# Moving w1's load behind the first tiles of x, two evacuations to VectorE, and splitting the last tile, in a one-core token-mixer and MLP kernel

## The chip, the cores and the metric

The kernel runs on one core of one Trainium2 chip. The metric is device microseconds of that core: the median of repeated executions, lower is better. A trace covers the span of one execution, some 1.8 us less than its time (155.1 of 156.92 us in the traced run of the changed kernel). The granted clock is the share of TensorE's full clock that the profile says was granted. PE is TensorE, PEld its weight loads, DVE is VectorE, ACT is ScalarE, POOL is GpSimd, SP is SyncE; in a timeline "SPq" and "ACTq" are DMA issues of those engines.

## The reference

```python
B, S, D, F = 1, 2048, 512, 1792                  # x, w1..w4 in bf16
h  = gelu(layernorm(x) @ w1)
# four channel groups of h are shifted along S by +1, -1, +2, -2 and put together again: hs
x1 = x + hs @ w2
out = x1 + gelu(layernorm(x1) @ w3) @ w4
```

## The kernel before

x is worked on in 16 tiles of 128 rows. In layer 1 each tile goes through these steps: statistics on DVE (bn_stats, bn_aggr), 1/sqrt of the variance (tiles 0 to 3 on ACT and DVE; later pairs of tiles on GpSimd as `vpe` and `rstd`), normalization on DVE (`norm`), transposition on PE (`htp`), and evacuation of the transposed tile out of PSUM, into which the kernel has PE write, into `xnT` (`hev`). Four such tiles feed one group of PE matmuls (`yg`), whose result ACT copies out of PSUM; DVE then does most of the gelu. The kernel gives each engine its list in a fixed order. The order is worked out when the kernel is built, from estimated durations:

```python
class Sched:
    def add(self, eng, name, fn, reads=(), writes=(), dur=100.0, queue=None): ...
    def merge(self): ...   # list scheduling by `dur`; gives one order, waits are put in from reads and writes
```

These are the loads and their gates. `after` names what must be done before the load is issued:

```python
add_w_dma("act", "w1", w1_sb, w1, D * D * 2)               # ACT's queue, first of all
for t in range(min(4, NT)):
    add_x_dma("sp", t, 1)                                  # tiles 0..3, one load each
for k in range(1, NST):
    add_x_dma("sp", 4 * k, 4)                              # tiles 4..7, 8..11, 12..15
add_w_dma("pool", "w2", w2_sb, w2, D * D * 2, after=[(("xT", min(5, NT - 1)), 1)])
add_w_dma("pool", "w3", w3_sb, w3, D * F * 2, after=[(("xT", NT - 1), 1)])
add_w_dma("pool", "w4", w4_sb, w4, D * F * 2, after=[(("x1", ORDER2[min(4, NT - 1)]), 0)])
```

So w2 is issued by GpSimd, in its ordinary instruction list, once the evacuation of tile 5 is done. In that list it stands ahead of the `vpe` and `rstd` of tiles 8 and 9.

The evacuation of transposed tiles, and the last stage (14 matmuls for each tile, evacuation with the residual on DVE, store):

```python
def add_head_evac(t):
    ...
    sc.add("act", f"hev{t}", lambda e: e.activation(xnT[:, :, P * t : P * (t + 1)], src, ACT_F.Copy),
           reads=res, writes=[(("xT", t), 1)], dur=600)
# mm4: o_ps[128x512] = sum over 14 of h2T(fc).T @ w4(fc); then o_sb = o_ps + x1 on DVE; then the store from SP
```

## Time and profile before

| | before |
|---|---|
| time, median | 159.43 us (159.11 to 160.69, 16 runs) |
| span of the traced run | 157.7 us |
| busy: PE, DVE, ACT, POOL | 86%, 78%, 57%, 13% |
| granted clock | 1.0 |

The busy shares are averages over stages with different limits. The next lines are from the busy table over stretches of the kernel before. Its columns are the stretch in us, its length, the busy us of each engine (with the number of instructions), the granted clock, the busy share of the DMA engines, and GB/s.

```profile
8.00:26.00 18.00, 15.31 (x97) 7.71 (x99) 16.19 (x47) 12.30 (x21) 7.07 (x13) 1.00 0.18 69
26.00:62.00 36.00, 30.91 (x143) 13.33 (x147) 34.72 (x87) 25.75 (x35) 10.80 (x18) 1.00 0.54 141
62.00:85.00 23.00, 20.89 (x94) 8.80 (x93) 22.58 (x25) 20.35 (x17) 0.00 (x1) 1.00 0.16 32
85.00:152.00 67.00, 66.47 (x303) 30.02 (x309) 45.40 (x55) 29.70 (x25) 0.00 (x0) 1.00 0.08 28
```

From 26 to 85 us DVE is busy 57.3 of 59 us and sets the pace. From 85 us on it is PE, busy 66.5 of 67 us. Between 8 and 26 us DVE is busy 16.2 of 18 us; most of what is missing there is one wait. The waits of DVE in the kernel before (columns: who waited for whom, us in total, times, longest):

```profile
DVE o_sb L527 <- PE o_ps L612: 23.1, 11, 2.6
DVE st L376 <- DMA x_sb<-in_x_dram: 5.1, 2, 4.0
DVE xn_buf L425 <- POOL rstd L416: 2.2, 3, 1.4
```

The first line belongs to the end, where DVE has time. The second, 5.1 us for x tiles, lies in the first 6 us, before DVE has anything to work on. The third, 2.2 us for `rstd`, lies where DVE sets the pace. The head of the kernel before as a timeline (start us, duration, engine, line, operation, out<-in, count, and in brackets the idle time before it and what ended it):

```profile
4.04 0.69 DVE L376 BATCH_NORM_STATS2 st<-x_sb 128x6 f32<-128x512 bf16 x1 [4.04 <-DMA x_sb<-in_x_dram]
5.80 0.69 DVE L376 BATCH_NORM_STATS2 st<-x_sb 128x6 f32<-128x512 bf16 x1 [1.07 <-DMA x_sb<-in_x_dram]
...
8.08 0.38 DVE L425 TENSOR_SCALAR xn_buf<-x_sb,mv,rstd 128x512 bf16<-128x512 bf16 x1
...
9.56 1.28 DVE L376 BATCH_NORM_STATS2 st<-x_sb 128x6 f32<-128x512 bf16 x2
...
11.42 3.35 PE L574 MATMUL y_ps<-xnT,w_sb 128*128 128x512 bf16 x8 [0.90 <-ACT xnT L558]
...
17.12 0.96 POOL L350 DMA_DIRECT2D w_sb<-in_w_dram  x1 [2.86 <-ACT xnT L558]
...
18.11 0.25 POOL L411 TENSOR_SCALAR vpe<-mv 128x2 f32<-128x2 f32 x1
...
18.44 0.72 POOL L416 TENSOR_TENSOR rstd<-vpe,neghalf 128x2 f32<-128x2 f32 x1
...
19.19 0.74 DVE L425 TENSOR_SCALAR xn_buf<-x_sb,mv,rstd 128x512 bf16<-128x512 bf16 x2 [1.38 <-POOL rstd L416]
```

Tile 0 lands at 4.04 us. Tile 1 was issued 0.46 us later and is used 1.76 us later. The first norm starts at 8.08 us, the statistics of tile 4 at 9.56 us, the first y matmuls at 11.42 us; those eight matmuls take 3.35 us. GpSimd gets to issue w2 at 17.12 us, after 2.86 us of waiting for the evacuation of tile 5. Only then does it compute the `rstd` of tiles 8 and 9, and DVE idles 1.38 us for it.

### The profile page before, as it was taken

How to read it: one execution, taken by the hardware profiler on the slowest of the kernel's cores; microseconds unless marked ns; L12 is line 12 of the kernel's file. 1: busy time of each engine (PE TensorE's matmuls, PEld its weight loads, DVE VectorE, ACT ScalarE, POOL GpSimd, SP SyncE). 2: the span in 40 equal slices, each digit the busy share in tenths (PEclk: the TensorE clock that was granted, in tenths of full speed). 3: DMA queues.
4: the chain of work that ended last, by engine and by line, in shares of the span. 5: the costliest groups of instructions: out<-in, count | busy, mean ns of one | idle time of the engine just before them, and what ended most of it. 6: DMA issues, size and time to landing. Idle time of an engine off the chain costs nothing.

```text
span 157.7 us, 1812 instructions
## 1 busy us (share of the span) xinstructions
PE 136.3 (86%) x643; PEld 60.9 (39%) x656; DVE 123.0 (78%) x220; ACT 89.9 (57%) x98; POOL 19.7 (13%) x46
## 2 busy tenths in 40 slices
PE   0069889659969999995999999999999999999992
PEld 0044344214324444442443444444444444444440
DVE  0799699999999998999999999613999938922311
ACT  3074777979956555789896979610687742200000
POOL 4013642200144446000000000000000000000000
PEclk9999999999999999999999999999999999999999
DMA  5940120480069845530000010001000010110010
GB/s 148 325 192 0 48 85 6 111 354 0 2 205 294 170 70 100 100 63 0 0 2 0 0 35 2 0 33 37 34 33 0 0 67 33 37 67 33 33 66 34
DMA packets 13433, 11.12 MB, mean 70 GB/s; under 512 B 9137, under 2 KB 12209, under 8 KB 13425
## 3 DMA queue, kind: packets, MB, share of 16 engines
q1 hardware_dynamic: 12016, 6.29, 15.3%
q0 software_dynamic: 880, 4.19, 7.8%
q10 hardware_dynamic: 528, 0.52, 1.0%
q8 instruction: 5, 0.08, 0.2%
q14 instruction: 4, 0.02, 0.1%
HBM read 6.82 MB, written 2.10 MB: 57 GB/s over the span
## 4 chain that ended last, share of the span: by engine, by line
PE 44%; DVE 12%; issue 3%; ACT 2%; POOL 1%; POOLq 1%
PE o_ps L612 30%; PE y_ps L574 13%; DVE ub L477 3%; DVE x2b L462 3%; DVE h2T L497 2%; ACT ysb L449 2%; DVE x2b L469 2%; DVE xn_buf L425 1%; POOL vpe L411 1%; POOLq L728 1%; DVE st L376 1%; DVE o_sb L527 0%; DVE mv L381 0%; ACT sgb L484 0%
## 5 line engine op out<-in xcount | busy, mean ns | idle before, releaser
L574 PE MATMUL y_ps<-xnT,w_sb 128*128 128x512 bf16 x283 | 66.0, 385 | 5.1 <-ACT ysb L449 3.8
L612 PE MATMUL o_ps<-w_sb,h2T 128*128 128x512 bf16 x218 | 48.5, 379 | 0.3
L449 ACT ACTIVATE ysb<-y_ps 128x1024 bf16<-128x1024 f32 x36 | 35.6, 1018 | 18.5 <-DVE h2T L497 12.1
L484 ACT ACTIVATE sgb<-ub 128x1024 bf16<-128x1024 bf16 (+1 forms) x24 | 35.6, 1485 | 14.1 <-DVE ub L477 14.1
L574 PEld LDWEIGHTS y_ps<-xnT,w_sb 128*128 128x128 bf16 x288 | 27.3, 99 | 40.5 <-issue 5.1
L612 PEld LDWEIGHTS o_ps<-w_sb,h2T 128*128 128x128 bf16 x224 | 21.9, 98 | 26.4
L527 DVE TENSOR_TENSOR o_sb<-o_ps,x_sb 128x512 bf16<-128x512 f32 x16 | 11.0, 690 | 23.2 <-PE o_ps L612 23.1
L376 DVE BATCH_NORM_STATS2 st<-x_sb 128x6 f32<-128x512 bf16 x32 | 20.3, 672 | 5.1 <-DMA x_sb<-in_x_dram 5.1
L477 DVE TENSOR_TENSOR ub<-x2b,ysb 128x1024 bf16<-128x1024 bf16 (+1 forms) x24 | 23.0, 958 | 0.8
L462 DVE TENSOR_TENSOR x2b<-ysb 128x1024 bf16<-128x1024 bf16 (+1 forms) x24 | 22.8, 951 | 0.2
L497 DVE TENSOR_TENSOR h2T<-ysb,sgb 128x2048 bf16<-128x2048 bf16 (+1 forms) x16 | 17.2, 1085 | 0.0
L594 PE MATMUL o_ps<-w_sb,hT 128*128 128x512 bf16 x62 | 16.0, 379 | 0.1
L469 DVE TENSOR_SCALAR x2b<-x2b 128x1024 bf16<-128x1024 bf16 (+1 forms) x24 | 13.6, 565 | 0.8
L425 DVE TENSOR_SCALAR xn_buf<-x_sb,mv,rstd 128x512 bf16<-128x512 bf16 x32 | 11.7, 408 | 2.4 <-POOL rstd L416 2.2
L548 PE MATMUL o_ps<-ident,xn_buf 128*128 128x128 bf16 x56 | 5.1, 231 | 9.7 <-DVE xn_buf L425 8.5
L519 ACT ACTIVATE x_sb<-o_ps 128x512 bf16<-128x512 f32 x16 | 9.5, 597 | 5.8 <-PE o_ps L594 5.7
L416 POOL TENSOR_TENSOR rstd<-vpe,neghalf 128x2 f32<-128x2 f32 x14 | 10.5, 753 | 1.2
L558 ACT ACTIVATE xnT<-o_ps 128x512 bf16<-128x512 bf16 x14 | 7.6, 597 | 2.5 <-PE o_ps L548 2.3
L594 PEld LDWEIGHTS o_ps<-w_sb,hT 128*128 128x128 bf16 x64 | 6.3, 98 | 6.9
L590 PE MATMUL o_ps<-x_sb,ident 128*128 128x512 bf16 x16 | 6.1, 382 | 3.2 <-DVE hT L512 3.2
L548 PEld LDWEIGHTS o_ps<-ident,xn_buf 128*128 128x128 bf16 x56 | 3.7, 102 | 12.7 <-DVE xn_buf L425 9.5
L411 POOL TENSOR_SCALAR vpe<-mv 128x2 f32<-128x2 f32 x14 | 4.5, 320 | 20.3 <-DVE mv L381 20.3
(21 smaller groups left out, 24.0 us busy)
## 6 DMA issues: line engine op xcount, KB each, us to landing
w_sb<-in_w_dram POOLq DMA_DIRECT2D x2, 1792.0 KB, 8.3
out_dram<-o_sb SPq DMA_DIRECT2D x16, 128.0 KB, 1.8
x_sb<-in_x_dram SPq DMA_DIRECT2D x3, 512.0 KB, 6.7
w_sb<-in_w_dram ACTq DMA_DIRECT2D x1, 512.0 KB, 4.7
x_sb<-in_x_dram SPq DMA_DIRECT2D x4, 128.0 KB, 4.4
w_sb<-in_w_dram POOLq DMA_DIRECT2D x1, 512.0 KB, 4.3
xnT<-xn_buf SPq DMA_TRANSPOSE x16, 2.5
```

The lines of the kernel that those rows point to most:

```text
L376: sc.add("dve", f"bnst{gt}", lambda e: e.bn_stats(st6[:, gt, :], src), reads=[(rsrc, 0)], writes=[(("st6", gt), 0)], dur=650)
L425: lambda e: e.tensor_scalar(xn_buf[:, gt % NXN, :], src, mv[:, gt, 0:1], rstd[:, gt : gt + 1], ALU.subtract, ALU.mult),
L449: lambda e: e.activation(ysb[:, u % NYS, GW * h : GW * (h + 1)], y_ps[:, 512 * b : 512 * b + GW], ACT_F.Copy),
L462: lambda e: e.tensor_tensor(x2b[:, u % NX2, 0:W], y, y, ALU.mult),
L469: lambda e: e.tensor_scalar(x2, x2, GELU_K, None, ALU.add),
L477: lambda e: e.tensor_tensor(ub[:, u % NUU, 0:W], x2b[:, u % NX2, 0:W], y, ALU.mult),
L484: lambda e: e.activation(sgb[:, u % NSS, 0:W], ub[:, u % NUU, 0:W], ACT_F.Sigmoid, scale=GELU_C2),
L497: sc.add("dve", f"c4_{u}", lambda e: e.tensor_tensor(dst, y, sg, ALU.mult), reads=rd, writes=w, dur=90 + 0.54 * W)
L527: lambda e: e.tensor_tensor(o_sb[:, k % NO, :], o_ps[:, 512 * (k % 2) : 512 * (k % 2 + 1)], x1_sb[:, t, :], ALU.add),
L574: ins = e.matmul(dst, wsb[:, dc, P * fc : P * (fc + 1)], srcT[:, dc, 512 * st : 512 * (st + 1)], start=(dc == 0), stop=(dc == DC - 1))
L594: ins = e.matmul(dst, hT[:, j, c0 : c0 + P], w2_sb[:, j, :], start=False, stop=(j == DC - 1))
L612: ins = e.matmul(dst, h2T[:, fc, st2 % 2, P * q : P * (q + 1)], w4_sb[:, fc, :], start=(fc == 0), stop=(fc == FC - 1))
```

## The change

The intent is a quicker head and a shorter tail: x tiles should not load beside w1 (in the kernel before, the first four took 4.4 us from issue to landing by the median; in the changed one 2.5); the first four transposed tiles should be evacuated by two engines, so that PE starts earlier; the last tile is done in two halves, so that only half of it has to be evacuated and stored after the last matmul. Most waits for stores are also taken before the end. The diff, cut to what is switched on:

```diff
-            add_w_dma("act", "w1", w1_sb, w1, D * D * 2)
...
-            for k in range(1, NST):
+            add_x_dma("sp", 4, 2)
+            add_w_dma("sp", "w1", w1_sb, w1, D * D * 2)
+            add_x_dma("sp", 6, 2)
+            for k in range(2, NST):
                 add_x_dma("sp", 4 * k, 4)
...
+            if DEV["dve_head_evac"] and t < 4 and t % 2 == 1:
+                sc.add("dve", f"hev{t}", lambda e: e.tensor_copy(dst, src),
+                       reads=res, writes=[(("xT", t), 1)], dur=400)
+            else:
+                sc.add("act", f"hev{t}", lambda e: e.activation(dst, src, ACT_F.Copy), ...)
...
+            if k2 == NT - 1 and DEV["split_last"]:        # matmuls, evacuation and store of the last tile
+                for h in (0, 1):                          # in two halves of 256 columns, each in its own PSUM bank
+                    add_mm4(k2, half=h)
...
+            if k2 >= 3 and half is None:                  # SP: wait for store k2-3 right after issuing store k2
+                sc.add("sp", f"ow{k2}", lambda e: e.nop(),
+                       reads=[(("outdma", k2 - 3, None), 0)], dur=50)
...
-                   writes=[(("y", gs), g)], dur=4 * 235 + 60)
+                   writes=[(("y", gs), g)], dur=(1780 if layer == 1 and st == 0 else 4 * 235 + 60))
```

The last hunk is an estimate only, but estimates make the order. PE transposes tiles 8 to 11 one group of matmuls earlier, and DVE normalizes tiles 8 and 9 before the statistics of tile 13 instead of after them. The diff also adds several switches that are off.

## The prediction

> **What bounds the kernel now.** Span 157.7 us, granted clock 1.0. The busy table over stretches gives three regimes. (1) 0 to 8 us: loading; the VectorE (DVE) waits 4.04 us for x tile 0 and 1.07 us for tile 1 (waits view). (2) 9.6 to about 85 us: DVE is 90 to 98% busy and sets the pace; its only idle stretches are 1.38 + 0.19 us at 19 to 20 us and 0.60 us at 62 us, all waiting for rstd from GpSimd. (3) 85 to 155 us: PE is gapless (matmuls of 512 columns every 0.216 us). Then 0.69 us of evacuation and about 2.2 us of store. The chain of waits agrees. So a microsecond won on DVE before 79 us, or in the tail, should be a microsecond of time.
>
> **What the change does**:
> - w1 leaves the ACT queue, and goes behind x tiles 0 to 5 on SP's queue. [...] slices 1 and 2 run at 325 and 192 GB/s, and tile 1 lands 1.7 us after tile 0 although the issues are 0.46 us apart. Estimate: tile 1 lands about 1.5 us earlier, so norms start near 6.6 us instead of 8.08.
> - Two of the first four transposed-tile evacuations move from ACT (0.57 us each) to DVE. DVE must wait for the fourth tile's transposes, about 2.05 us after the first norm in this trace, then copy (0.45 us, estimate). xT is complete near 9.4 instead of 11.3 us, so the first y matmuls start about 1.8 us earlier. But DVE returns to its statistics at about 9.4 instead of 9.56 us: on DVE the head gain is nearly eaten.
> - The earlier PE makes the evacuation of tile 5 earlier (16.85 to about 15 us). The w2 load on GpSimd waits for it (2.86 us wait, issue until 18.08) and holds up the rstd of tiles 8 and 9, for which DVE idles 1.38 us. I expect this stall to shrink to 0 to 0.4 us. Main gain: about 1.3 us, with the head's rest.
> - The last tile is split into halves of 256 columns: PE work equal (28 x about 0.108 us; the weight load hides), last evacuation about 0.4 instead of 0.69 us, last store half as large. Gain about 0.35 us.
> - Earlier waits for stores on SP: nothing; the last landing rules (1.0 us wait).
> - The altered estimates reorder PE's transposes of tiles 8 to 15 and three DVE operations; no work added. The stall at 62 us stays.
>
> **Prediction.** 159.49 - 1.3 - 0.35 = 157.8 us, range 156.8 to 158.9. Faster by over 2% (below 156.3): 0.07; within 2%: 0.91; slower: 0.02.
>
> **What would show it.** DVE's second statistics start near 4.3 us (was 5.80), first norm near 6.6 us; first y matmul near 9.5 us (was 11.42); DVE idle before the norm of tile 8 under 0.4 us (was 1.38); DVE then ahead by 1.0 to 1.7 us, and that lead unchanged at 46, 62 and 85 us; last evacuation 0.4 us; end of PE to end of span 0.3 us shorter.
>
> **What would make it wrong.** x tiles that land no earlier; w1 landing after 9.5 us, so the first matmuls wait for it; a DVE lead lost in a new wait on ACT or PE between 26 and 62 us; 256-column matmuls slower than half of a 512-column one; or a tail store whose landing time does not depend on size.

## The result

| | before | changed |
|---|---|---|
| time, median | 159.43 us (159.11 to 160.69, 16 runs) | 157.05 us (156.43 to 157.87, 11 runs) |
| ratio | | 0.9848, 95% interval 0.9825 to 0.9871 |
| span of the traced run | 157.7 us | 155.1 us |

Ratios are the mean time of one kernel's runs over that of the other's in the same rounds, so they are not quite the ratios of the medians. The change wins 2.4 us, 1.5%, which is clear of the noise. Its runs scatter more: of the kernel before, 15 of 16 runs lie within 0.8 us, and of the changed one they fill 1.4 us evenly. The head of the changed kernel, in the same view as before:

```profile
2.96 1.38 DVE L392 BATCH_NORM_STATS2 st<-x_sb 128x6 f32<-128x512 bf16 x2 [2.96 <-DMA x_sb<-in_x_dram]
...
5.92 0.38 DVE L456 TENSOR_SCALAR xn_buf<-x_sb,mv,rstd 128x512 bf16<-128x512 bf16 x1
...
8.40 0.42 DVE L633 COPY xnT<-y_ps 128x512 bf16<-128x512 bf16 x1 [0.43 <-PE y_ps L621]
...
8.74 1.27 DVE L392 BATCH_NORM_STATS2 st<-x_sb 128x6 f32<-128x512 bf16 x2
...
8.92 3.39 PE L664 MATMUL y_ps<-xnT,w_sb 128*128 128x512 bf16 x8 [0.56 <-DVE xnT L633]
...
14.66 0.96 POOL L356 DMA_DIRECT2D w_sb<-in_w_dram  x1 [1.23 <-ACT xnT L636]
...
16.74 0.73 DVE L456 TENSOR_SCALAR xn_buf<-x_sb,mv,rstd 128x512 bf16<-128x512 bf16 x2 [0.34 <-POOL rstd L432]
```

Set beside the lines of before, DVE's lead is 1.08 us at the first statistics, 2.16 at the first norm (5.92 for 8.08), only 0.82 at the statistics of tile 4 (8.74 for 9.56), because of the two copies and the 0.43 us of waiting for PE before the second, and 2.45 at the norm of tile 8, where 1.38 us of idling (the stall, from here on) has become 0.34. The statistics of tile 13 were done before that norm in the old order and come after it in the new one. Counting that, the lead at the statistics of tile 14 is 2.17 us (18.78 for 20.95). From there on it doesn't move. These are DVE's wait for the last `rstd` and the last PE wait before the end stage, first before, then after:

```profile
62.04 0.74 DVE L425 TENSOR_SCALAR xn_buf<-x_sb,mv,rstd 128x512 bf16<-128x512 bf16 x2 [0.60 <-POOL rstd L416]
```
```profile
85.20 1.89 PE L574 MATMUL y_ps<-xnT,w_sb 128*128 128x512 bf16 x8 [0.16 <-ACT ysb L449]
```

```profile
59.87 0.74 DVE L456 TENSOR_SCALAR xn_buf<-x_sb,mv,rstd 128x512 bf16<-128x512 bf16 x2 [0.60 <-POOL rstd L432]
```
```profile
83.03 1.89 PE L664 MATMUL y_ps<-xnT,w_sb 128*128 128x512 bf16 x8 [0.15 <-ACT ysb L493]
```

The lead is 2.17 us at both. The last evacuation, before and after:

```profile
154.81 0.69 DVE L527 TENSOR_TENSOR o_sb<-o_ps,x_sb 128x512 bf16<-128x512 f32 x1 [2.33 <-PE o_ps L612]
```

```profile
151.15 0.42 DVE L600 TENSOR_TENSOR o_sb<-o_ps,x_sb 128x256 bf16<-128x256 f32 x1 [0.84 <-PE o_ps L709]
152.67 0.42 DVE L600 TENSOR_TENSOR o_sb<-o_ps,x_sb 128x256 bf16<-128x256 f32 x1 [1.10 <-PE o_ps L709]
```

It takes 0.42 instead of 0.69 us. From its start the span lasted 2.9 us more before (157.7 - 154.81) and 2.4 us after (155.1 - 152.67), so about 0.45 us is won here, of which 0.27 is evacuation; the rest is the smaller last store (by the median 1.5 us from issue to landing for 64 KB, 1.8 for 128).

### The profile page after: what moved, and what is told of

Read it like the earlier page. It is cut to its first block, busy times and chain, and to the rows that moved or that the text cites. A ratio compares the mean times of both kernels' runs of the same rounds, so it can differ in the third digit from the quotient of the medians.

```text
span 155.1 us, 1856 instructions
## 1 busy us (share of the span) xinstructions
PE 136.7 (88%) x658; PEld 62.2 (40%) x670; DVE 123.8 (80%) x223; ACT 88.9 (57%) x96; POOL 19.7 (13%) x46
## 4 chain that ended last, share of the span: by engine, by line
PE 45%; DVE 12%; issue 3%; ACT 2%; POOL 1%; POOLq 1%
PE o_ps L709 31%; PE y_ps L664 14%; DVE ub L541 4%; DVE x2b L517 3%; DVE h2T L562 2%; ACT ysb L493 2%; DVE x2b L526 2%; DVE xn_buf L456 1%; POOL vpe L427 1%; POOLq L845 1%; DVE st L392 1%; DVE o_sb L600 0%; DVE mv L397 0%; ACT sgb L549 0%
## 5 line engine op out<-in xcount | busy, mean ns | idle before, releaser
L709 PE MATMUL o_ps<-w_sb,h2T 128*128 128x512 bf16 (+1 forms) x233 | 48.6, 366 | 0.3
L709 PEld LDWEIGHTS o_ps<-w_sb,h2T 128*128 128x128 bf16 x238 | 23.3, 98 | 25.3
L600 DVE TENSOR_TENSOR o_sb<-o_ps,x_sb 128x512 bf16<-128x512 f32 (+1 forms) x17 | 11.2, 659 | 22.8 <-PE o_ps L709 22.7
L636 ACT ACTIVATE xnT<-o_ps 128x512 bf16<-128x512 bf16 x13 | 7.1, 592 | 1.6 <-PE o_ps L621 1.5
```

What stands on the lines that cost most here:

```text
L600: lambda e: e.tensor_tensor(o_sb[:, k % NO, cols], src, x1_sb[:, t, cols], ALU.add),
L709: ins = e.matmul(dst, h2T[:, fc, st2 % 2, P * q : P * (q + 1)], w4_sb[:, fc, cols], start=(fc == 0), stop=(fc == FC - 1))
```

## Experiments

Theory T arose from the two traces: the lead is made by the landing of the x tiles alone, and the copies on DVE and the shortened stall cancel. Rival R is the attribution in the prediction: the copies and the earlier PE make the larger part. To keep every other instruction in its place, the order was in most runs built unaltered and the named operation moved afterwards; where the edit comes before the order is made (w1 alone) or is a switch, the traces show the instructions of each engine in the same order but for the listed edits.

| run | time, median (runs) | ratio to before, same rounds |
|---|---|---|
| w1 moved, nothing else | 157.35 (157.31 to 158.41, 6) | 0.9880 |
| changed, w1 back on ACT | 158.30 (158.02 to 158.86, 6) | 0.9930 |
| changed, no copies on DVE | 157.34 (157.30 to 157.77, 6) | 0.9870 |
| changed, last tile not split | 157.40 (156.80 to 158.22, 6) | 0.9867 |
| changed, w2 on SP | 156.42 (156.34 to 156.82, 5) | 0.9828 |
| changed, w2 on SP, no copies | 155.30 (155.15 to 155.89, 4) | 0.9759 |
| before, w2 on SP | 158.35 (158.25 to 159.13, 6) | 0.9954 |
| combined | 154.94 (154.52 to 156.02, 6) | 0.9736 |
| changed, again | 156.98 (156.45 to 157.38, 6) | 0.9854 |
| changed, idle matmuls first | 156.07 (156.03 to 156.81, 5) | 0.9808 |
| changed, waits for stores at the end | 156.95 (156.29 to 158.08, 6) | 0.9856 |
| before, again | 159.41 (1) | |

All gave correct results. The rows fall into three batches of four, each on another chip; the kernel before took 159.38, 159.15 and 159.34 us in them. The 157.05 us of the changed kernel come from rounds of their own (ratio 0.9848), so differences of 0.3 us to them are within the noise of the times, and are read from the traces.

### w1 moved, and nothing else

```diff
-            add_w_dma("act", "w1", w1_sb, w1, D * D * 2)
-            for k in range(1, NST):
+            add_x_dma("sp", 4, 2)
+            add_w_dma("sp", "w1", w1_sb, w1, D * D * 2)
+            add_x_dma("sp", 6, 2)
+            for k in range(2, NST):
                 add_x_dma("sp", 4 * k, 4)
```

> The kernel before with one edit: w1 goes behind x tiles 0 to 5 on SP's queue; every other instruction stays in the order of before. Theory T (the lead is made by the x tiles' landing alone; the two DVE copies cost DVE 1.3 us and give it back as a shorter stall, net about nothing): everything up to the end shifts earlier by the 2.16 us by which the first norm moved (8.08 to 5.92), the stall before the norm of tile 8 stays at 1.4 us, DVE statistics of tiles 14 and 15 start near 18.8 us as in the changed kernel, time near 157.3 us (ratio 0.986). Rival R (the copies and the earlier PE make the larger part of the gain, as the prediction put it): the lead at 21 us is 1 us or less and the time is above 158.2 us.

Measured: 157.35 us, 2.03 us less than before in the same rounds. From the timelines of DVE and GpSimd in this run:

```profile
5.82 0.38 DVE L425 TENSOR_SCALAR xn_buf<-x_sb,mv,rstd 128x512 bf16<-128x512 bf16 x1
...
9.34 1.29 DVE L376 BATCH_NORM_STATS2 st<-x_sb 128x6 f32<-128x512 bf16 x2 [0.54 <-DMA x_sb<-in_x_dram]
...
15.09 0.96 POOL L350 DMA_DIRECT2D w_sb<-in_w_dram  x1 [2.56 <-ACT xnT L558]
...
17.17 0.73 DVE L425 TENSOR_SCALAR xn_buf<-x_sb,mv,rstd 128x512 bf16<-128x512 bf16 x2 [1.08 <-POOL rstd L416]
...
18.92 1.25 DVE L376 BATCH_NORM_STATS2 st<-x_sb 128x6 f32<-128x512 bf16 x2
```

The lead at the statistics of tile 14 is 2.03 us (18.92 for 20.95), as large as the gain in time. The stall before the norm of tile 8 is still there with 1.08 us. T expected 157.3 us, R more than 158.2. So the load's move alone makes nearly all of the lead, and most of the stall stays where it was. It fell by 0.3 us only because DVE now waits 0.54 us at another place, for x tile 6, which comes behind w1. At the last `rstd` near 60 us the lead of this run is 2.16 us (59.88 for 62.04), the same as that of the whole change (2.17).

### The changed kernel with w1 back on ACT's queue

```diff
+        o = by["dma_w1"]           # after the order is made
+        o.eng = o.queue = "act"
+        sc.order.remove(o)
+        sc.order.insert(0, o)
```

> The changed kernel with w1 put back to the head of ACT's queue; all else in the changed kernel's order. T: the whole head shifts back by about 2.2 us, the DVE copies alone give nothing before the tail (DVE statistics of tiles 14 and 15 near 21 us, stall before the norm of tile 8 about 0.3 us), what remains against before is the tail: time near 159.0 us (ratio 0.997). R: the copies and the shorter stall keep 1 us or more: time 158.3 us or less.

Measured: 158.30 us, 1.1 us less than before. T expected 159.0, R at most 158.3. T misses by 0.7 us; R's limit is just met. The trace (of the fastest of the six runs, 158.02 us):

```profile
3.47 0.69 DVE L392 BATCH_NORM_STATS2 st<-x_sb 128x6 f32<-128x512 bf16 x1 [3.47 <-DMA x_sb<-in_x_dram]
```
```profile
10.48 2.78 PE L664 MATMUL y_ps<-xnT,w_sb 128*128 128x512 bf16 x8 [0.56 <-DVE xnT L633]
```

Tile 0 landed 0.57 us earlier here than in the trace of before, PE's first eight matmuls took 2.78 us instead of 3.35, and DVE did not wait for `rstd` of tile 8 at all. The first two differ from one execution to the next (3.47 to 4.04 us and 2.78 to 3.57 us where w1 is on ACT's queue), and here both helped; how much of the miss of the median they explain is not shown. So everything but the move of w1 is worth 1.1 us by itself, 0.45 us of it in the tail. With the 2.0 us of the first experiment that makes 3.1 us, but both together win only 2.4. The parts overlap. Both bring the evacuation of tile 5 forward, and the stall behind it can be removed only once; that reading is argued from the traces, and the next experiments test it.

### The changed kernel without the copies on DVE

```diff
+        for t in (1, 3):           # after the order is made
+            o = by[f"hev{t}"]
+            o.eng = "act"          # and its function becomes ACT's copy
```

> The changed kernel with the evacuations of tiles 1 and 3 back on ACT, all else in the changed kernel's order. T: DVE reaches the statistics of tile 4 1.3 us earlier (near 7.4 us), but xT is complete 0.3 us later (near 9.1 us), so the w2 issue on GpSimd and the norm of tile 8 come 0.3 us later and the stall grows to about 1.9 us; time 0 to 0.4 us above the changed kernel's, 157.0 to 157.4 us. R: without the copies more than 0.8 us is lost (157.9 us or more). A third view, that the copies are pure cost on the engine that sets the pace, would have it 1.3 us faster (155.8 us).

Measured: 157.34 us, 0.3 us more than the changed kernel (ratio 0.9870 against 0.9848; the intervals overlap). DVE and GpSimd in this run:

```profile
7.25 1.28 DVE L392 BATCH_NORM_STATS2 st<-x_sb 128x6 f32<-128x512 bf16 x2
...
15.02 0.96 POOL L356 DMA_DIRECT2D w_sb<-in_w_dram  x1 [3.07 <-ACT xnT L636]
...
17.10 0.73 DVE L456 TENSOR_SCALAR xn_buf<-x_sb,mv,rstd 128x512 bf16<-128x512 bf16 x2 [2.18 <-POOL rstd L432]
```

DVE is at the statistics of tile 4 at 7.25 us, 1.5 us before the changed kernel, and then idles 2.18 us before the norm of tile 8. Whatever DVE gains ahead of that point, GpSimd takes back. The 0.8 us of copies and 0.43 us of waiting on DVE are paid out of this idle time, and their profit is that PE starts 0.3 us sooner after the first norm (3.00 us after it in the changed kernel, 3.34 here). The norm of tile 8 starts 0.36 us later here (17.10 for 16.74).

The traces show what times DVE at this point. In all eight of them in which DVE waits here, the norm of tile 8 starts 2.07 or 2.08 us after GpSimd starts the w2 issue (19.19 and 17.12 us before, 16.74 and 14.66 changed, 17.17 and 15.09 with w1 alone, 17.10 and 15.02 here). So as long as there is a stall, a part of the change is worth what it brings that issue forward, and not what it saves on DVE ahead of it.

One more part shows here, which had no run of its own: the new order. This run and that of w1 alone load x and w1 alike and both evacuate on ACT. They differ by the split tail, the waits for stores and the order, and take the same time (157.34 and 157.35 us), although the tail gains about 0.45 us (next run). At the norm of tile 8 this run is 0.07 us ahead, at the statistics of tile 14 it is 0.23 us behind (19.15 for 18.92), and near 60 us 0.35 us (60.23 for 59.88). The old order did the statistics of tile 13 (0.69 us) during the stall, the new one does them behind it. So the new order seems to cost about 0.3 us, as much as the copies gain.

### The changed kernel with the last tile in one piece

The edit is one switch: `"split_last": True` becomes `False`.

> The changed kernel with the last tile not split. All views: the head is the same. If the tail gain is the shorter last evacuation (0.69 to 0.42 us) plus a smaller last store (0.15 to 0.2 us), the time is 0.4 to 0.5 us above the changed kernel's (157.5 us) and last matmul to end of span is 0.45 us longer. If the tail's gain were only in the evacuation, 0.27 us.

Measured: 157.40 us, 0.35 us more than the changed kernel in its own, other rounds; the scatter of 1.4 us makes this rough. The trace is firmer:

```profile
152.80 0.69 DVE L600 TENSOR_TENSOR o_sb<-o_ps,x_sb 128x512 bf16<-128x512 f32 x1 [2.33 <-PE o_ps L709]
```

From the start of this last evacuation the span lasts 2.9 us more (it ends at 155.7), against 2.4 us in the changed kernel. So the tail is worth about 0.45 us.

### w2 issued by SP behind x, so that GpSimd is free

```diff
+        o = by["dma_w2"]           # after the order is made; in the changed kernel and in the one before
+        o.eng = o.queue = "sp"
+        o.reads = []               # nothing to wait for: it follows the last x load on the queue
+        sc.order.remove(o)
+        sc.order.insert(sc.order.index(by["dma_x12"]) + 1, o)
```

In the changed kernel:

> The changed kernel with w2 issued behind x on SP's queue instead of on GpSimd behind the evacuation of tile 5; all else in the same order. T (the stall before the norm of tile 8 is GpSimd held up by the w2 issue, which hangs on PE's first matmuls): the stall of 0.34 us vanishes, rstd of tiles 8 and 9 comes at least 0.5 us before it is needed, time 156.7 us or a little less; and as DVE no longer hangs on PE's first 8 matmuls, the spread of the runs falls from 1.4 us to 0.7 us or less. Rival (the stall and the spread come from the landing of the x tiles): no change in either.

Measured: 156.42 us, and five runs lie within 0.48 us. The stall is gone. This supports T's account of it: GpSimd, held by the w2 issue.

The same without the copies on DVE:

> The same with the evacuations of tiles 1 and 3 back on ACT. T: with GpSimd free there is no stall left for the copies to shorten, so they are pure cost on DVE: the time falls by another 0.7 to 1.3 us to 155.4 to 156.0 us (DVE may wait some 0.5 us for x tile 6, as it did in the run with w1 alone). Rival (the copies help by starting PE earlier, which matters by itself): the time stays or rises above 156.7 us.

Measured: 155.30 us, 1.12 us less than the run before it, in the same rounds. DVE here:

```profile
7.41 1.28 DVE L392 BATCH_NORM_STATS2 st<-x_sb 128x6 f32<-128x512 bf16 x2
...
14.99 0.72 DVE L456 TENSOR_SCALAR xn_buf<-x_sb,mv,rstd 128x512 bf16<-128x512 bf16 x2
```

The norm of tile 8 starts at 14.99 us without any wait. Together with the third experiment this settles what the copies are: a small gain, about 0.3 us, where DVE had to wait for GpSimd anyway, and a loss of 1.1 us where it had not. The rival, that an earlier PE start matters by itself and not only through the w2 issue, falls.

In the kernel before:

> The kernel before with w2 issued behind x on SP's queue, nothing else. T: its two stalls of 1.38 and 0.19 us on DVE vanish and the time falls by 1.3 to 1.6 us, to 158.0 us (ratio 0.991). Rival: the stall only moves to the next wait and the time stays above 159.0 us.

Measured: 158.35 us, a gain of 0.8 us where 1.3 to 1.6 were expected. The wait for `rstd` vanishes, but a new one opens later:

```profile
17.20 0.72 DVE L425 TENSOR_SCALAR xn_buf<-x_sb,mv,rstd 128x512 bf16<-128x512 bf16 x2
...
26.55 0.83 DVE L512 TENSOR_TENSOR hT<-ysb,sgb 128x512 bf16<-128x512 bf16 x3 [0.95 <-ACT sgb L484]
```

DVE now waits 0.95 us for ACT's sigmoid, which stands behind evacuations of transposed tiles in ACT's list. Part of the stall only moved, so the rival is partly right for the old order. The changed kernel's order with w2 on SP shows no such wait.

### A combination

```diff
+        # the edits of w2 on SP and of no copies on DVE, as above, and:
+        o = by["dma_w1"]           # behind x tiles 6 and 7
+        sc.order.remove(o)
+        sc.order.insert(sc.order.index(by["dma_x6"]) + 1, o)
+        o = by[f"c2b_{NU1}"]       # a multiplication of layer 2's first gelu unit, ahead of the last two norms
+        sc.order.remove(o)
+        sc.order.insert(sc.order.index(by[f"norm{2 * NT - 2}"]), o)
```

> The run without copies and with w2 on SP, with two more edits: w1 goes one place further back, behind x tiles 6 and 7, and the gelu multiplication of the first unit of layer 2 goes ahead of the last two norms on DVE, which wait 0.60 us for rstd in both kernels. T: DVE waits no more for x tile 6, the wait of 0.60 us near 60 us vanishes, PE's first matmuls start later (w1 lands near 9.4 us) at no cost; time 154.7 to 155.2 us (ratio 0.972). If PE's own limit holds from 46 us on, the 0.60 us is not won and the time is 155.3 to 155.8 us.

Measured: 154.94 us, ratio 0.9736 to before; as its six runs reach up to 156.02, the further gain over the previous 155.30 is not firm. The wait of 0.60 us near 60 us is gone. But in the traced run, one of the slower ones at 155.24 us, tile 2 landed late:

```profile
5.06 0.69 DVE L392 BATCH_NORM_STATS2 st<-x_sb 128x6 f32<-128x512 bf16 x1 [0.59 <-DMA x_sb<-in_x_dram]
```

DVE lost 0.59 us there, by chance about as much as the other edit won. This version has the lowest median of all run here and beats both kernels clearly.

### The changed kernel again, with PE kept busy early, and with late waits for stores

These ask why the changed kernel scatters. The first has no edit, the second is one switch (`"pe_warm": 0` becomes `7`, seven matmuls whose result is never used), the third takes the waits for stores back to the end.

> The changed kernel once more, unedited, for a second trace and for a comparison in the same rounds as the two runs beside it. Theory S (its runs spread over 1.4 us because a stretch of PE's first 8 matmuls, each 0.43 us at first and 0.22 us later, falls now before and now after the change of rate, and GpSimd, and through it DVE, hangs on them): in this trace the 8 matmuls take between 2.7 and 3.6 us, and the norm of tile 8 starts earlier or later by the same amount; time 156.4 to 157.9 us. Rival (the x tiles' landing): the 8 matmuls take 3.4 us as in the first trace and the head shifts as a whole.

> The changed kernel with its own switch for 7 idle matmuls on PE set, which run while x tiles are loading (tile 0 lands near 2.9 us; 7 x 0.43 us end near 6.0 us, before the first transposes at 6.4); all else in the same order. S: PE changes to the full rate before its first 8 real matmuls, which take 1.9 to 2.6 us instead of 3.4; GpSimd issues w2 earlier by as much, the stall of 0.34 us goes, time 156.3 to 156.7 us, and the spread falls to 0.7 us or less. Rival: no change in time or spread.

> The changed kernel with the waits for stores all at the end again, as before. Both views of the main gain are untouched. The last landing rules the end, so nothing changes: within 0.2 us of the changed kernel of the same rounds.

Measured: 156.98, 156.07 and 156.95 us. PE's timeline in the three runs, in this order:

```profile
9.19 3.59 PE L664 MATMUL y_ps<-xnT,w_sb 128*128 128x512 bf16 x8 [0.57 <-DMA w_sb<-in_w_dram]
```

```profile
3.38 3.17 PE L645 MATMUL y_ps<-x_sb,ident 128*128 128x512 bf16 x7 [3.38 <-DMA x_sb<-in_x_dram]
...
9.22 1.89 PE L664 MATMUL y_ps<-xnT,w_sb 128*128 128x512 bf16 x8 [0.57 <-DVE xnT L633]
```

```profile
9.98 3.47 PE L664 MATMUL y_ps<-xnT,w_sb 128*128 128x512 bf16 x8 [1.46 <-DMA w_sb<-in_w_dram]
```

GpSimd's w2 issue with the idle matmuls:

```profile
14.04 0.96 POOL L356 DMA_DIRECT2D w_sb<-in_w_dram  x1 [0.30 <-ACT xnT L636]
```

With the idle matmuls the first eight real ones take 1.89 instead of about 3.5 us, GpSimd issues w2 at 14.04 us, DVE's stall is gone, and four of the five runs lie within 0.1 us, 0.9 us below the changed kernel of the same rounds. So PE's slow start does reach the time, through GpSimd. But theory S was not the whole of it: in the other two traces the last thing that PE waited for was w1 itself. In the first of them that made nearly no difference (0.57 us, where DVE's copy alone makes it 0.56 to 0.57), but in the other PE waited 1.46 us, as w1 landed only just before 9.98 us. In that run (158.08 us, the slowest) the norm of tile 8 starts at 17.88 us after 1.11 us of idling:

```profile
17.88 0.73 DVE L456 TENSOR_SCALAR xn_buf<-x_sb,mv,rstd 128x512 bf16<-128x512 bf16 x2 [1.11 <-POOL rstd L432]
```

At least two things therefore scatter the changed kernel, the landing of w1, which now comes just as PE is ready for it (at 8.89 us in the first trace, where a weight load waited for it, with the matmuls following at 8.92), and the moment at which PE's rate about doubles (eight matmuls took 3.39 us at 8.92 us in the first trace, and 1.89 at 83.03); both act by way of the w2 issue. The rival, the landing of the x tiles, isn't ruled out: in the trace of the changed kernel again the norm of tile 8 starts 0.47 us later than in the first one (17.21 for 16.74), and 0.26 us of this are there at the first norm (6.18 for 5.92). How much of the scatter is due to each stays open. The waits for stores change nothing, as expected: 156.95 against 156.98 us.

### The kernel before again

No edit; one run with a trace.

> The kernel before once more, for a second trace of the landing of its x tiles: tile 0 at 4.04 us in the first trace, but 3.47 and 3.52 us in the two experiments that issued w1 in the same way. If the first trace was late by chance, tile 0 lands near 3.5 us and the true head gain of w1's move is nearer 1.6 than 2.16 us; the stall before the norm of tile 8 is then 1.4 us again.

Measured: 159.41 us.

```profile
3.81 0.69 DVE L376 BATCH_NORM_STATS2 st<-x_sb 128x6 f32<-128x512 bf16 x1 [3.81 <-DMA x_sb<-in_x_dram]
...
19.18 0.73 DVE L425 TENSOR_SCALAR xn_buf<-x_sb,mv,rstd 128x512 bf16<-128x512 bf16 x2 [1.60 <-POOL rstd L416]
```

Tile 0 landed at 3.81 us, so the expectation of 3.5 us was missed, and 4.04 in the first trace was not far out. Over all traces the first norm starts at 7.48 to 8.08 us where w1 is on ACT's queue (four traces, mean 7.74) and at 5.76 to 6.25 us where it is behind tiles 0 to 5 (nine traces, mean 6.00). So w1's move brings the first norm forward by 1.7 us on average; the 2.16 us of the first pair lies on the high side. DVE reaches the norm of tile 8 at 19.18 us here and at 19.19 in the first trace, although it started 0.24 us earlier: the stall is 1.60 instead of 1.38 us and has taken the difference.

## Why the prediction was right, and where its reasons were not

The time of 157.05 us lies in the range of 156.8 to 158.9, and the forecast "within 2%" holds. The gain was 2.4 us where the prediction's sum gave 1.65 (1.3 in the head and stall, 0.35 in the tail). The head and stall were the term that was sized too small: DVE's lead became 2.17 us. The time lies near the lower end of the range, and three of the 11 runs lie below it, so the hit owes something to the width of the range.

- **What bounds the kernel: right.** DVE's lead is 2.17 us at 21 us, at 62 us and at 85 us, with no new wait between, and it reaches the end unchanged. A microsecond won early on DVE was a microsecond of time.
- **w1's move: right in direction, the mis-sized term.** The norms were put near 6.6 us and started at 5.92, a lead of 2.16 us in this pair of traces and 1.7 us on average, against 1.5 expected. DVE was to be back at the statistics of tile 4 with 0.16 us of lead ("at about 9.4 instead of 9.56 us: on DVE the head gain is nearly eaten"); it had 0.82 (8.74 us).
- **The copies' cost: right.** 0.42 us each (0.45 was the author's estimate), and DVE does wait for the fourth tile, 0.43 us. First y matmul at 8.92 us (9.5 expected).
- **The stall: right in size, wrong in what it was worth.** It fell from 1.38 to 0.34 us as predicted, through the named path. But calling this the "main gain: about 1.3 us" was wrong as an attribution. With w1 moved alone, no copies and the stall still 1.08 us, 2.03 of the 2.4 us are there. The shorter stall in the main only paid for the copies: taking these away loses 0.3 us. The prediction booked w1's move and the copies as one sum on DVE up to 9.5 us and credited the stall separately, whereas both meet in the same wait. The path was the right one, and read from its end it gives more: the prediction moved the evacuation of tile 5, and with it the w2 issue, by about 1.85 us (16.85 to about 15); the issue moved by 2.46 us (17.12 to 14.66) and took the norm of tile 8 with it.
- **The tail: right, slightly undersized.** The evacuation took 0.42 us as estimated, and the smaller store brought the term from 0.35 to about 0.45 us. The halves cost PE nothing visible: the lead at the last matmul's end is 2.13 us, against 2.17 at 85 us.
- **Waits for stores: right.** Nothing was expected and nothing was found.
- **The new order: not free.** The prediction has "no work added", which is right, but the order seems to cost about 0.3 us (see the run without the copies).
- **Half foreseen:** the scatter. The prediction names a w1 that lands after 9.5 us as what could spoil it; in one trace (9.98 us) that happened. That this would make the times of the runs differ was not said.

## What to carry to other kernels

Before crediting a shortened wait, ask what else ends at that wait: work put on the waiting engine can hide in it (here 1.3 us of copying and waiting for PE cost nothing), and becomes a loss once the wait's real cause is removed (here a DMA issue placed in the instruction list of an engine that also feeds the critical one). Test each part of a change alone and all but that part: here 2.0 and 1.1 us alone gave 2.4 together, and the version with the lowest median kept the early x tiles and the split but dropped the copies. A load that the first tile doesn't need belongs behind that tile (here the first norm started at 6.00 instead of 7.74 us on average), yet not so far back that its landing decides when the next engine starts (as at 9.98 us in one trace), where that start matters. And where a reordering comes along with a change, ask what used to be done for free during a wait.

## What these traces show of the hardware

- PE is slow at first. In the second trace of the kernel before, PE began transposing at 8.28 us, and all eight matmuls up to 14.76 us (11.19 plus 3.57) were still at the slow pace, 6.5 us later, with pauses of at most 0.9 us between; even the four at 15.41 us took 1.86 us, where four fast ones take 1.03. With the idle matmuls from 3.38 us on the eight at 9.22 us were all fast (1.89 us). The profile's granted clock, 1.00 from 8 to 15 us in that second trace, does not show it. What sets the moment of the change is not shown.
- Over the whole time the idle matmuls were worth 0.6% (156.07 against 156.98 us). It came by way of GpSimd's w2 issue (14.04 us, with DVE's stall gone), although PE had slack (in the first trace of the changed kernel it was busy 15.18 of the 18 us from 8 to 26 us).
- A 512 KB load issued beside four tiles of 128 KB delays the first norm from 6.00 to 7.74 us on average. By what mechanism is not shown.
- In the kernel before, the 128x2 `vpe` takes 0.22 us at 57.42 us and 1.28 us at 59.50 us, beside a TENSOR_TENSOR of DVE of 1.23 us. That the one slows the other, and that this is part of the wait of 0.60 us near 60 us, is argued; no run tested it.
- What decided most in this case: a DMA issue that waits in GpSimd's list held up the small GpSimd work behind it (2.86 us of waiting and 0.96 us of issue before the `rstd` of tiles 8 and 9).
